# A one-core transformer block with a hand-kept order of work: one input load moved to GpSimd's DMA queue, and a new order list

## The chip, the cores and the metric

The kernel runs on one core of one Trainium2 chip. A core has TensorE (PE in the profile, with its weight loads PEld), VectorE (DVE), ScalarE (ACT), GpSimd (POOL) and SyncE (SP), each with its own instruction stream; they meet through semaphores. SP, ACT and GpSimd can issue DMA transfers, which run on the core's 16 DMA engines. The metric is the device time of one execution in microseconds (us); lower is better.

## The reference

A transformer block on x of 2048 tokens by 640 features, in bfloat16: layer norm, a memory-augmented linear and softmax attention of 32 heads of 20 features in 4 segments of 512 tokens, a residual, layer norm again, and a two-layer network with SiLU of 1728 hidden features.

```python
phi = lambda t: jnp.where(t > 0, t + 1.0, jnp.exp(t))
for s in range(N):                       # N = 4 segments of L = 512 tokens
    logits = einsum('bhqd,bhkd->bhqk', qs, ks) * scale + mask
    a_dot = einsum('bhqk,bhkd->bhqd', softmax(logits), vs)
    num = einsum('bhld,bhde->bhle', phi(qs), M)
    den = einsum('bhld,bhd->bhl', phi(qs), z)[..., None] + 1e-06
    outs.append(g * num / den + (1.0 - g) * a_dot)
    M = M + einsum('bhld,bhle->bhde', phi(ks), vs)
    z = z + einsum('bhld->bhd', phi(ks))
h = x + concat(outs) @ wo                # q, k, v from layernorm(x)
h2 = h + silu(layernorm(h) @ w1) @ w2
```

## The kernel before

The tokens are 16 blocks of 128 (x_tok holds 12 of them at a time), 4 blocks to a segment. Every piece of work is a task that `build` declares with what it reads and writes. `Graph.schedule` doesn't choose an order: it follows the text `ORDER` (line 360 on), a list of some 1,480 entries. An entry is a task's name, after a slash the engine where the task may run on several (A for ACT, D for DVE, G for GpSimd, S for SP), and after a colon the buffer places that it takes, such as the PSUM banks. Each engine executes its tasks in the order of the list, and `Tracker` puts a semaphore wait ahead of an instruction wherever an earlier task of another engine has to be done. So the list sets for every engine what stands behind what. The list was written by a search that works with a cost for each task; the kernel holds its result alone.

Names that matter here (the first digit after a name is the segment or the block, x and y are the first and the second half of segment 0):

- x0, x1, x2 (blocks 2 and 3 in one transfer), x4, x8: loads of x, line 577. w_q0, w_q1, w_k0, w_k1, w_wv0, w_wv1: loads of the projection weights, each in a part of 384 rows (0, from SP) and one of 256 rows (1, from ACT), line 580. beta: a small load with 128 copies, line 592.
- zpad, w2z, warm, halfc, epsc, epsg, mt, mta, mtb, mm, mzc, vpad: constants and masks, mostly on GpSimd. iota (line 629, GpSimd) and sel (line 631, DVE) make the identity matrix for transposes.
- fillN: N matmuls on zeros that only keep PE running (line 617).
- n1_st, n1_r, n1_ap: statistics (lines 737 and 740 on ACT, 745 and 748 on DVE), reciprocal root (lines 756 to 766) and application (line 772) of the first layer norm; n2_ the same for the second. n1_tp and n1_te (lines 781, 790): transpose on PE and its eviction in segment 0, called te0 to te3 below; n1_tr: transpose by DMA later.
- re_q, re_k (lines 695 and 697): the weights of q and k laid out by heads, in five parts c.
- pr, qe (lines 859, 867 and 868): projection of q (third digit 0) or k (1), and its eviction. ex, pha, phb (lines 874, 881, 887): phi.
- vt (line 899): twelve transfers that gather the heads of groups 5 to 7 from the projections into a place of their own.
- v, ve (lines 824, 834, 835): projection of v and its eviction.
- qk, e, mk (lines 936, 947, 958): scores of a group of four heads, the exponential, the causal mask. av, oe (lines 979, 992, 994): product with v and eviction. tn, nm (lines 1008, 1012, 1025 to 1045): transpose back, division. kt, mz, ma, mb: the memory M.
- ot, wo, rs (lines 1154, 1162, 1170): output projection and residual. h1, th, s (lines 1197, 1206, 1212) and h2, o, out (lines 1239, 1252, 1257): the network and the store.

SP's queue at the start issues x0, w_q0, w_k0, w_wv0, x4, w_wo, beta and then the weights of the network; ACT's queue issues x1, w_q1, x2, w_k1, w_wv1. The twelve vt go out on SP, some on ACT. The scores of groups 5, 6 and 7 in the first half (qk5x0, qk6x0, qk7x0) need all twelve; in the list, qk7x0 is the first of them, and v02 follows it on PE.

Which queue a load may take is an argument of its call:

```python
def load_x(b0, n, prio, bw=2.1, kind="plain", engs=(SP, AC)):
    s0 = b0 % 12
    dma(f"x{b0}", [], [(X[b], [0]) for b in range(b0, b0 + n)],
        lambda e: e.dma_start(out=x_tok[:, s0:s0 + n, :], in_=xv[:, b0:b0 + n, :]), prio, bw, kind, engs=engs)
```

Of the kernel before, what the change touches and what calls it, by code (L numbers as in the profile page):

```python
# [1314 lines left out]
```

## Time and profile before

| what | us |
|---|---|
| median of 3 runs (303.77 to 304.54) | 304.46 |
| the profiled execution, its own time | 305.88 |
| its span, first to last instruction | 304.1 |
| PE busy, of the span | 289.5 (95%) |
| ACT busy | 225.4 (74%) |
| DVE busy | 222.4 (73%) |
| GpSimd busy | 141.8 (47%) |

The granted clock of TensorE over the whole span is 0.994 of full speed. PE is the engine with the most work; matmuls are pipelined and their ends are modelled, so its busy time also holds short waits. Over the span of 304.1 us the page's slices show how PE and the clock stand, each digit a fortieth of the span in tenths:

```profile
PE   7799789999999999899999999999999999999996
...
PEclk9999799999999999999999999999999999999999
```

PE is below nine tenths in the first two slices, in the fifth and sixth (30.4 to 45.6 us), in the seventeenth and in the last; the clock is at 7 in the fifth (30.4 to 38.0 us). A row of the chain of waits (followed back from the last instruction) names the line and how long it held the chain; there PE has 73% of the span, DVE 11%, ACT 9%, and a DMA 3%, the load of wk at the start.

### The profile page before, as it was taken

Reading aid. Unit: us, or ns where it says so; the run is one execution under the profiler, and the core shown is the slowest. Engines: PE = TensorE matmul, PEld = TensorE weight load, DVE = VectorE, ACT = ScalarE, POOL = GpSimd, SP = SyncE. Lnnn points to the kernel's source line nnn. Section 1 sums busy time; section 2 is a strip of 40 time slices with the busy share of each in tenths; the row PEclk is TensorE's granted clock in tenths of the full one; section 3 lists DMA queues with packets and bytes.
Section 4 is the critical chain, followed back from the end, with each engine's and each line's share of the span. In section 5 each row is a group of like instructions: output and inputs, shape, how many; then the busy total and the mean of one; then the engine's idle time right before and its main releaser. Section 6 shows DMA issues by size and latency. Waiting matters only on the chain.

```text
span 304.1 us, 7512 instructions
## 1 busy us (share of the span) xinstructions
PE 289.5 (95%) x2989; PEld 171.4 (56%) x3011; DVE 222.4 (73%) x506; ACT 225.4 (74%) x326; POOL 141.8 (47%) x273
## 2 busy tenths in 40 slices
PE   7799789999999999899999999999999999999996
PEld 6575445465655555556654454466565547764574
DVE  5899777977749889989759876767874786745613
ACT  5899698999999899888679989886879841005400
POOL 7589543434545546765546437382855430300000
PEclk9999799999999999999999999999999999999999
DMA  7997415405344210151342300233230013240001
GB/s 264 358 369 118 87 24 138 114 19 162 72 101 95 43 34 10 34 107 27 64 134 76 67 19 19 39 64 75 65 68 24 0 20 68 45 122 9 0 30 58
DMA packets 48754, 24.66 MB, mean 81 GB/s; under 512 B 39184, under 2 KB 47632, under 8 KB 48720
## 3 DMA queue, kind: packets, MB, share of 16 engines
q1 hardware_dynamic: 46108, 21.06, 29.1%
q10 hardware_dynamic: 2612, 3.12, 3.6%
q8 instruction: 24, 0.39, 0.5%
q14 instruction: 10, 0.08, 0.1%
HBM read 10.41 MB, written 2.62 MB: 43 GB/s over the span
## 4 chain that ended last, share of the span: by engine, by line
PE 73%; DVE 11%; ACT 9%; DMA 3%; issue 2%; ACTq 1%; DVEq 0%
PE ps_all L1239 20%; PE ps_all L1197 16%; PE ps_all L859 9%; PE ps_all L824 7%; PE ps_all L936 6%; PE ps_all L1162 6%; ACT PT L947 6%; PE ps_all L979 4%; DMA sT<-in_A_wk_dram 3%; PE ps_all L1008 2%; PE ps_all L1101 2%; PE ps_all L1012 1%; DVE on L1045 1%; DVE sT L1212 1%; DVE x_tok L1170 1%
## 5 line engine op out<-in xcount | busy, mean ns | idle before, releaser
L947 ACT ACTIVATE PT<-ps_all 128x1024 bf16<-128x1024 f32 (+1 forms) x168 | 157.0, 990 | 17.2 <-PE ps_all L936 16.4
L958 POOL TENSOR_SCALAR_AFFINE_SELECT PT<-PT 128x512 bf16<-128x512 bf16 x128 | 82.4, 650 | 75.1 <-ACT PT L947 72.4
L1239 PE MATMUL ps_all<-w_sb,sT 128*128 128x320 bf16 (+2 forms) x462 | 64.6, 295 | 0.1
L1197 PE MATMUL ps_all<-hT,w_sb 128*128 128x512 bf16 (+1 forms) x315 | 60.3, 335 | 1.2 <-issue 1.0
L1206 ACT ACTIVATE th<-ps_all 128x512 f32<-128x512 f32 (+2 forms) x70 | 34.6, 510 | 34.2 <-PE ps_all L1191 19.6
L1239 PEld LDWEIGHTS ps_all<-w_sb,sT 128*128 128x128 bf16 x462 | 43.3, 98 | 19.2 <-issue 2.8
L1212 DVE SCALAR_TENSOR_TENSOR sT<-th,ps_all 128x512 bf16<-128x512 f32 (+2 forms) x70 | 37.8, 558 | 15.9 <-ACT th L1206 15.7
L1197 PEld LDWEIGHTS ps_all<-hT,w_sb 128*128 128x128 bf16 x325 | 29.9, 98 | 24.1 <-issue 2.6
L1252 DVE SCALAR_TENSOR_TENSOR x_tok<-ps_all,x_tok 128x640 bf16<-128x640 f32 (+3 forms) x18 | 13.4, 747 | 22.6 <-PE ps_all L1239 22.3
L745 DVE BATCH_NORM_STATS2 stt<-x_tok 128x6 f32<-128x320 bf16 x62 | 27.0, 477 | 0.8 <-DMA x_tok<-in_A_x_dram 0.5
L766 POOL TENSOR_TENSOR rst<-rst,eps_c 128x1 f32<-128x1 f32 x32 | 18.4, 576 | 12.7 <-DVE rst L760 10.6
L1162 PE MATMUL ps_all<-wo_sb,oT 128*128 128x320 bf16 x160 | 23.9, 299 | 0.0
L979 PE MATMUL ps_all<-PT,Vx 128*32 128x256 bf16 (+3 forms) x576 | 23.3, 287 | 0.5 <-DVE Vx L835 0.5
L1053 POOL TENSOR_TENSOR otok<-on 128x320 bf16<-128x320 bf16 x24 | 19.3, 810 | 7.8 <-DVE on L1045 7.8
L772 DVE TENSOR_SCALAR xn_rot<-x_tok,mvt,rst 128x640 bf16<-128x640 bf16 x32 | 15.7, 495 | 6.6 <-POOL rst L766 5.9
L868 DVE CAST QK<-ps_all 128x512 bf16<-128x512 f32 x24 | 16.5, 687 | 5.4 <-PE ps_all L859 5.1
L1045 DVE TENSOR_TENSOR on<-ps_all,rd 128x640 bf16<-128x640 f32 x24 | 19.8, 824 | 0.8
L1162 PEld LDWEIGHTS ps_all<-wo_sb,oT 128*128 128x128 bf16 x160 | 14.8, 98 | 7.2 <-issue 2.0
L824 PE MATMUL ps_all<-wv_sb,xT 128*128 128x320 bf16 x120 | 18.3, 299 | 0.3 <-ACT Vx L834 0.3
L979 PEld LDWEIGHTS ps_all<-PT,Vx 128*32 128x32 bf16 x576 | 12.2, 96 | 10.9 <-issue 4.1
L859 PE MATMUL ps_all<-xT,wqr 128*128 128x512 bf16 x68 | 17.2, 380 | 1.2 <-DVE x_tok L1170 0.7
L859 PE MATMUL ps_all<-xT,wkr 128*128 128x512 bf16 x70 | 17.6, 380 | 0.6 <-DVE sT L1212 0.2
(90 smaller groups left out, 350.7 us busy)
## 6 DMA issues: line engine op xcount, KB each, us to landing
w_sb<-in_B_w_dram SPq DMA_DIRECT2D x5, 432.0 KB, 11.0
x_tok<-in_A_x_dram SPq DMA_DIRECT2D x3, 640.0 KB, 10.5
out_dram<-x_tok SPq DMA_DIRECT2D x10, 160.0 KB, 1.8
w_sb<-in_B_w_dram SPq DMA_DIRECT2D x2, 480.0 KB, 3.8
wo_sb<-in_A_wo_dram SPq DMA_DIRECT2D x1, 800.0 KB, 12.3
out_dram<-x_tok ACTq DMA_DIRECT2D x5, 160.0 KB, 1.8
QKV<-QK SPq DMA_DIRECT2D x11, 72.0 KB
w_sb<-in_B_w_dram SPq DMA_DIRECT2D x1, 640.0 KB, 4.3
```

The lines of the kernel that those rows point to most:

```text
L745: T.add(DV, lambda e, hh=hh: e.bn_stats(out=stt[:, s, 6 * hh:6 * hh + 6], in_=xb[:, 320 * hh:320 * hh + 320]), reads=R((xa, xsub)), writes ...
L824: fns.append(lambda e, c=c, hh=hh: e.matmul(bank(ps, hh)[:, 0:320], lhsT=xT_[:, c, 128 * i:128 * i + 128], rhs=wv_sb[:, c, 320 * hh:320 * ...
L859: fns = [lambda e, kc=kc: e.matmul(bank(ps)[:, lo:hi], lhsT=wt[:, kc, c, :], rhs=xT_[:, kc, lo:hi], start=(kc == 0), stop=(kc == NC - 1)) ...
L947: T.add(AC, lambda e: e.activation(out=pt[:, pta.slot, q0:q0 + 2, 0:width], in_=sc3[:, b0:b0 + 2, 0:width], func=ACT.Exp, scale=SCALE), re ...
L958: T.add(PO, lambda e: e.affine_select(out=v, in_=v, pattern=[[0, 4], [1, 128]], compare_op=ALU.is_ge, fill=0.0, base=0, channel_multiplier ...
L979: fns.append(lambda e, j=j, r=r, h=h, pa=pa, pt=pt, co=co, q0=q0, ji=ji: e.matmul(bank(po)[32 * r:32 * r + 32, q0:hi], lhsT=Vx[:, vx.slot, ...
L1045: T.add(DV, lambda e: e.tensor_tensor(out=on[:, ona.slot, :, :].rearrange("p b (x e) -> p b x e", e=DH), in0=v[:, :, :, 0:DH], in1=r2.unsq ...
L1162: fns.append(lambda e, c=c, hh=hh: e.matmul(bank(ps, hh)[:, 0:320], lhsT=oT[:, c, 128 * i:128 * i + 128], rhs=wo_sb[:, c, 320 * hh:320 * h ...
L1197: fns = [lambda e, c=c: e.matmul(bank(ps)[:, lo:hi], lhsT=w1_sb[:, c, 128 * f:128 * f + 128], rhs=hT[:, c, lo:hi], start=(c == 0), stop=(c ...
L1206: T.add(AC, lambda e: e.activation(out=th[:, tha.slot, lo:hi], in_=bank(ps)[:, lo:hi], func=ACT.Tanh, scale=0.5), reads=R((ps, [0])), writ ...
L1212: T.add(DV, lambda e: e.scalar_tensor_tensor(out=sT[:, f, lo:hi], in0=th[:, tha.slot, lo:hi], scalar=1.0, in1=bank(ps)[:, lo:hi], op0=ALU. ...
L1239: fns.append(lambda e, f=f, t0=t0, fr=fr, hh=hh, n=n: e.matmul(bank(pa, hh)[:, 0:n], lhsT=sT[:, f, t0:t0 + 128], rhs=w2_sb[:, fr, c0 + 320 ...
```

## The change

The load of x2 and x3 (blocks 2 and 3, 320 KB) is issued by GpSimd in place of ACT; it is GpSimd's first task. The whole list is replaced by another result of the search, in which the issue times of transfers are taken as they were measured, and in which VectorE and GpSimd take their turns in order of time. The tasks are the same ones, except for the filler matmuls: 55 in four groups in place of 38 in three. What changes is their order on each engine, the engine of tasks that can run on several (n1_st0, for one, moves from ACT to DVE, and oe goes to ACT 8 times in place of 14), and the PSUM banks and other places. The diff of the list is cut to its start, as far as qk7x0, and its end.

```diff
--- before.py
+++ after.py
@@ -358,108 +358,108 @@
      "x0": -0.6, "xs": 0.4, "y0": 3.0, "ys": 0.65, "wox": 3.6, "h1x": 5.0}
 
 ORDER = """
-x1:3 mt1:0 mt0 halfc x0:7 w_q1:0 x2:5,0 mta0 mtb0 mm2 mm9 w_q0 w_k0 mt3 w_wv0:0 x4:1,2,4,6 iota w_wo:0 beta w2z/D:0
-zpad w_w2_4 w_w1_2:0 w_w1_4 w_w2_5 epsc sel mta3 vpad1 w_k1 w_wv1 x8/S:8,9,10,11 warm n1_st0/A:1,0 vpad0 mtb3 mm8
-n1_st1/D:6 n1_r1/D n1_ap1:1 mta1 w_w1_1 re_wq1/A:0 re_wq0/D n1_r0/G n1_ap0:0 re_wq2/D epsg0 n1_st3/D:0 mtb1 mm3 mt2
-mta2 mm11 mm1 n1_r3/G mtb2 n1_st2/D:2 n1_r2/D n1_ap3:2 re_wk1/D:0 n1_ap2:3 w_w1_0 w_w1_3 re_wk4/D re_wk3/D re_wq3/D
-fill6:0 fill27:1 fill5:2 mm7 mm6 mm4 mm5 mm10 mm0 n1_tp1:0 n1_te1/A:0 re_wk2/D n1_tp0:4 n1_te0/A pr020x:7 pr000x:2
-pr010x:0 re_wq4/A n1_tp3:3 re_wk0/A pr001x:5 qe000x/A:0 qe010x/A:0 qe020x/A:0 n1_te3/A qe001x/A n1_tp2:0 n1_te2/A
-pr011x:2 qk0x0:3 pr040y:7 pr001y:0 qe011x/D e0x0:0 e0x2 mk0x_0 qe001y/D qe040y/A:0 qk1x0:1 e1x0:1 pha001:2 mk0x_256
-e1x2 mk1x_0 pr021x:5 qe021x/D pr041y:6 qe041y/A pr031y:0 n1_st5:3 n1_r5/G n1_st4:7 n1_r4/G n1_ap5:3 n1_tr5:0
-qe031y/A:0 ex001:1 phb001 kt00:1 mk1x_256 pr030x:1 qe030x/A qk2x0:4 e2x2:2 zf0 zf1 mzc10 mzc0 mzc8 mzc9 mzc6 mzc4 mzc5
-mzc3 lsc0 mzc2 pr041x:2 pr031x:3 qe031x/D qe041x/D e2x0 pha031:1 mzc1 lsc1 mk2x_0 pha041:0 n1_ap4:1 mzc7 epsg1 mzc11
-ex031:1 mk2x_256 pr040x:0 qe040x/A pr030y:1 qe030y/D vt07/S:0 vt011/S vt02/S n1_st6:5 vt01/S lsc2 lsc3 n1_r6/G vt08/S
-n1_st11:2 n1_r11/G n1_st10:0 qk3x0:2 e3x2:3 pr010y:6 e3x0 pr011y:7 qe011y/D phb031 vt05/A n1_ap6:0 n1_st7:4 mk3x_0
-mk3x_256 n1_ap11:2 qe010y/A n1_st9:1 n1_r10/G pr000y:0 qe000y/A qk4x0:2 e4x2:5 pr021y:1 vt04/A pr020y:6 qe021y/A
-pha021:2 e4x0 mk4x_0 qe020y/A mk4x_256 ex041:0 vt00/S vt06/S v00:4 ve00/A:0 qk0yb0:0 e0yb2:4 vt09/A v01:6 n1_r9/D
-vt010/S e0yb0 vt03/A ve01/A mk0yb_0 ex011:2 n1_r7/G n1_tr6 n1_tr4 v03:4 ve03/D qk1yb0:0 e1yb0:6 av0x:6 oe0x/D:1 av4x:4
-av2x:7 e1yb2 mk1yb_0 mk1yb_256 tn0x:0 oe4x/D:0 oe2x/D:1 ex021:1 phb021 kt02:0 nm0x:0 n1_st8:6 n1_ap7:1 n1_tr7 qk7x0:1
-e7x0:2 v02:5 n1_r8/D n1_ap9:0 phb041 tn4x:7 nm4x:0 e7x2 mk7x_0 mk7x_256 ve02/A qk5x0:1 av1x:0 v11:5 e5x0:0 e5x2 mk5x_0
...
-s3_5_0 h2_15_0_2:2 th3_4_0:0 th3_10_0:1 s3_4_0 s3_10_0 h1_3_9_0:5 th3_9_0:1 s3_9_0 h1_3_7_0:4 th3_7_0:0 h1_3_8_0:1
-th3_8_0:1 h2_13_0:6 s3_7_0 h2_15_0_1:0 h2_15_1_1 s3_8_0 h2_15_2_1 h2_15_3_1 o15_1 out15_1/S h2_15_0_0:3 h2_13_1
-h2_13_2 h2_13_3 o13 out13/A h2_15_1_0 h2_15_1_2 h2_14_0:4 h2_14_1 h2_14_2 h2_12_0:0 h2_14_3 h2_12_1 o14 out14/S
-h2_12_2 h2_12_3 o12 out12/S h2_15_2_0 h2_15_3_0 o15_0 out15_0/S h2_15_2_2 h2_15_3_2 o15_2 out15_2/A
+x0:7 w_q0:0 x1:3 w_q1 x2:5,0 epsg0:0 mt2 mt0 zpad iota w_k0 w_wv0:0 vpad0 x4:1,2,4,6 w2z/D:0 mta0 mtb0 mm0 w_wo:0 beta
+w_w2_4 w_w1_1:0 w_w1_2 w_w1_4 halfc w_w1_0 w_k1 w_wv1 w_w2_5 sel warm n1_st0/D:1,0 w_w1_3 x8/S:8,9,10,11 n1_st1/D:6
+mm6 epsc n1_r0/G n1_ap0:0 mm2 re_wq1/D:0 n1_r1/G n1_ap1:1 mt3 mta3 n1_st3/D:0 mt1 mm9 n1_r3/G mta1 mtb1 mm5 n1_st2/D:2
+mm1 n1_r2/G mm4 mm3 mtb3 mm8 vpad1 mta2 re_wq0/A re_wq2/A mtb2 mm10 mm11 fill42:0 n1_tp0:2 n1_tp1:4 re_wk0/D:0
+n1_ap3:2 re_wq4/D n1_te1/A:0 n1_te0/A mm7 re_wk1/A re_wq3/D re_wk2/A re_wk4/A n1_ap2:3 fill10:1 pr000x:4 pr010x:1
+pr011x:0 qe011x/A:0 qe010x/D n1_tp3:2 n1_te3/D re_wk3/D n1_st5:3 n1_r5/G n1_st6:5 n1_r6/G n1_st4:7 n1_r4/G qe000x/A:0
+pr001x:5 qe001x/A pr020x:7 qe020x/A:0 n1_tp2:0 n1_te2/A qk0x0:2 e0x2:0 pr021x:6 e0x0 mk0x_0 qe021x/A pr001y:7 qe001y/A
+pha001:2 n1_ap5:3 n1_tr5:0 pr041y:0 qe041y/A:0 qk1x0:1 e1x0:1 ex001:1 phb001 lsc0 zf0 zf1 mzc9 mzc2 mzc0 mzc8 lsc1
+mzc3 mzc6 mzc5 mzc7 mk0x_256 mzc10 mzc1 pr030x:5 qe030x/D:0 mzc4 e1x2 kt00:1 n1_st7:4 mk1x_0 mk1x_256 mzc11 n1_ap6:0
+pr040y:6 pr030y:0 qe030y/A pr041x:7 qe041x/A pha041:0 pr031x:1 qe040y/A epsg1 qk2x0:2 pr031y:0 lsc2 e2x0:2 qe031y/A
+qe031x/A e2x2 mk2x_0 pr040x:7 qe040x/D vt02/S:0 pr010y:6 qk3x0:0 e3x0:3 e3x2 vt01/A mk2x_256 n1_st9:1 qe010y/D vt08/S
+vt07/S mk3x_0 mk3x_256 pr021y:7 vt010/S qe021y/D ex021:1 pr011y:4 vt05/S qe011y/D pr000y:5 qk4x0:0 e4x2:5 e4x0 mk4x_0
+vt04/A n1_st11:2 ex041:0 qe000y/D pr020y:4 qe020y/D vt00/S vt06/S n1_r11/G vt03/A vt09/S n1_st8:6 n1_r8/G n1_r9/G
+v00:6 ve00/D:0 mk4x_256 pha021:2 pha011:1 phb021 qk0yb0:2 e0yb0:4 v01:0 e0yb2 mk0yb_0 mk0yb_256 vt011/A ex011:2 kt02:0
+n1_tr6 n1_r7/D ve01/D v03:6 phb041 lsc3 ve03/D qk1yb0:2 e1yb0:6 av2x:1 av0x:0 oe0x/D:1 oe2x/D:0 av4x:7 e1yb2 mk1yb_0
+tn0x:6 nm0x:0 n1_ap4:1 n1_ap11:2 mk1yb_256 n1_st10:0 n1_ap7:3 qk7x0:0 v02:4 oe4x/A:1 tn4x:6 av1x:7 oe1x/D:1 n1_tr7
+e7x0:2 e7x2 mk7x_0 n1_ap9:0 mk7x_256 nm4x:0 n1_r10/G pha031:2 ve02/A qk5x0:0 e5x0:0 e5x2 v11:4 mk5x_0 mk5x_256 ex031:1
+n1_tr4 qk6x0:0 tn1x:7 phb011 e6x2:1 e6x0 mk6x_0 mk6x_256 nm1x:3 fill3:6 tn2x:6 nm2x:1 av7x:7 ve11/A:1 oe7x/D:1 av3x:6
...
+th3_5_0:1 s3_5_0 h1_3_6_0:4 th3_6_0:0 h1_3_8_0:5 th3_8_0:1 s3_6_0 h1_3_12_0:7 h2_14_0:0 h2_15_0_1:3 h2_15_1_1 s3_8_0
+h2_15_2_1 h2_15_0_2:2 th3_12_0:0 s3_12_0 h2_15_1_2 h2_15_3_1 o15_1 out15_1/A h2_14_1 h2_14_2 h2_14_3 o14 out14/S
+h2_13_0:4 h2_13_1 h2_13_2 h2_13_3 h2_15_0_0:6 o13 out13/S h2_12_0:0 h2_12_1 h2_12_2 h2_15_1_0 h2_12_3 o12 out12/S
+h2_15_2_0 h2_15_3_0 o15_0 out15_0/A h2_15_2_2 h2_15_3_2 o15_2 out15_2/S
 """.split()
@@ -582,7 +582,7 @@
     cw = lambda w: w.rearrange("(c p) e -> p c e", p=128)
     load_x(0, 1, -100, 2.30, "fix", (SP,))
     load_x(1, 1, -100, 2.33, "fix", (AC,))
-    load_x(2, 2, -97, 4.79, "fix", (AC,))
+    load_x(2, 2, -97, 4.79, "fix", (PO,))
     for wi, (k, A_w) in enumerate((("q", A_wq), ("k", A_wk))):
         load_w(k + "0", wraw[:, wi, 0:3, :], cw(A_w[0:384, :]), -99, 4.0, [(sT0, [k + "0"])], "fix", (SP,))
         load_w(k + "1", wraw[:, wi, 3:5, :], cw(A_w[384:640, :]), -99, 2.7, [(sT0, [k + "1"])], "fix", (AC,))
```

More of the change, by code (lines that the diff above doesn't have):

```diff
@@ new lines @@
+qk0ya0:0 e0ya2:5 oe3x/D:0 tn7x:7 nm7x:2 tn3x:4 nm3x:1 mz00:5 ma00/A:0 mb00:0 kt01:1 av5x:6 oe5x/D:0 av6x:7 e0ya0
+qk1ya0:2 oe6x/D:1 tn5x:6 nm5x:3 tn6x:7 nm6x:0 ot1:0 e1ya2:0 phb031 ot0 v10:0 ve10/D e1ya0 qk2ya0:4 e2ya0:2 av0y:2
+oe0y/D:1 v12:0 e2ya2 qk2yb0:2 e2yb0:1 w_w2_0/A ve12/D e2yb2 mk2yb_0 mk2yb_256 wo1:6 qk3ya0:0 e3ya2:3 rs1 n2_st1:5
+wo0:4 tn0y:7 nm0y:1 e3ya0 rs0 n2_st0:3 n2_r1/G n2_ap1:3 n2_tr1:0 n2_r0/G n2_ap0:1 n2_tr0 av1y:6 oe1y/A:0 qk4ya0:0
+pr101:7 v13:5 mz02:4 e4ya0:4 e4ya2 qe101/A:0 ma02/D:3 mb02:0 ve13/D pha101:1 ex101:2 phb101 qk3yb0:0 e3yb2:5 pr120:7
@@ new lines @@
+pha230:0 e16e0:5 e16e2 vt210/S vt24/S vt25/S vt211/S pha240:0 v22:6 ve22/D pha231:0 ex240:2 phb240 ex230:0 phb230
+vt22/S vt21/S vt28/S h1_0_13_1:0 th0_13_1:1 phb231 s0_13_1 mk16e_0 mk16e_256 qk17b0:2 e17b0:3 h1_0_11_1:1 th0_11_1:0
+s0_11_1 wo6:6 e17b2 mk17b_0 mk17b_384 qk18b0:0 e18b2:0 e18b0 mk18b_0 mk18b_384 rs6 ex220:0 av16:5 oe16/D:1 wo7:6
+n2_st6:6 qk17a0:2 e17a2:6 rs7 n2_r6/G n2_st7:4 e17a0 mk17a_0 wo4:0 rs4 n2_ap6:2 vt27/S ex241:2 h1_0_9_1:6 h1_0_3_1:7
+th0_9_1:1 th0_3_1:0 qk18e0:2 n2_r7/D s0_3_1 s0_9_1 wo5:0 e18e0:1 e18e2 mk18e_0 mk18e_256 phb220 n2_ap7:0 rs5
@@ new lines @@
+ad16 h1_1_7_0:3 th1_4_0:0 s1_4_0 phb241 th1_7_0:1 mk21b_384 s1_7_0 qk20a0:4 x12/S e20a2:0 e20a0 mk20a_0 h1_1_1_0:1
+n1_st12:0 h1_1_12_0:2 n1_r12/G th1_1_0:1 s1_1_0 th1_12_0:0 s1_12_0 n1_ap12:1 n1_tr12:0 mz23:0 qk20e0:3 h1_1_5_0:7 ma23
+e20e2:4 e20e0 mk20e_0 kt21:0 n1_st13:3 th1_5_0:1 h1_1_11_0:1 th1_11_0:0 n1_r13/G mk20e_256 s1_11_0 s1_5_0 qk21a0:3
+e21a2:1 e21a0 h1_1_2_0:2 th1_2_0:1 mk21a_0 n1_st14:6 n1_r14/G h1_1_6_0:0 th1_6_0:0 s1_2_0 n1_ap13:0 n1_tr13 n1_st15:1
+n1_ap14:2 n1_tr14 h1_1_8_0:1 qk22a0:4 e22a2:2 th1_8_0:1 s1_6_0 e22a0 v30:2 ve30/A:1 n1_r15/G n1_ap15:3 n1_tr15 mk22a_0
@@ new lines @@
+h1_1_0_0:6 th1_0_0:0 s1_8_0 s1_0_0 av21:7 av20:5 qk22b0:0 mz21:4 ma21 oe21/A:1 tn21:6 nm21:1,1 ad21 kt20:0 e22b0:3
+e22b2 mk22b_0 mk22b_384 oe20/D:1 h1_1_9_0:4 th1_9_0:1 s1_9_0 qk23a0:0 v32:6 ve32/D e23a0:6 e23a2 pr300:5 qk22e0:0
+e22e0:1 mk23a_0 qe300/D:0 pha300:0 e22e2 mk22e_0 mk22e_256 pr310:4 tn19:6 qe310/D:0 ex310:1 ex300:2 mz20:5 ma20
+pr301:0 qk23b0:2 e23b2:0 nm19:2,0 e23b0 mk23b_0 mk23b_384 phb300 mb20:0 pr311:1 ad19 qe301/D h1_1_3_0:7 th1_3_0:0
+kt24:0 tn20:5 qe311/D s1_3_0 qk24e0:1 e24e0:4 e24e2 mk24e_0 nm20:1,1 ad20 mk24e_256 pr320:0 pr330:7 v33:1 qe320/D:0
@@ new lines @@
+n2_ap13:3 n2_tr13:0 n2_ap14:2 n2_tr14 n2_ap15:1 n2_tr15 h2_8_1 h2_8_2 h2_8_3 wo12:4 o8 out8/A h2_9_0:0 rs12 n2_st12:7
+n2_r12/G h2_9_1 h2_9_2 h2_9_3 n2_ap12:0 n2_tr12 o9 h2_11_0:2 h2_11_1 h2_11_2 h2_11_3 o11 h2_10_0:0 h2_10_1 h2_10_2
+h2_10_3 out9/S h1_3_13_0:3 o10 out10/A out11/S th3_13_0:0 s3_13_0:0 h1_3_11_0:2 h1_3_0_0:5 th3_11_0:1 s3_11_0
+th3_0_0:0 h1_3_3_0:6 th3_3_0:1 s3_0_0 s3_3_0 h1_3_4_0:4 th3_4_0:0 s3_4_0 h1_3_9_0:0 th3_9_0:1 s3_9_0 h1_3_2_0:1
+h1_3_10_0:2 th3_2_0:1 h1_3_1_0:7 th3_1_0:0 s3_2_0 s3_1_0 th3_10_0:1 s3_10_0 h1_3_7_0:3 th3_7_0:0 s3_7_0 h1_3_5_0:6
```

136 lines of the change are left out of this document (55 added, 81 removed).

## The prediction

> **What bounds the kernel now.** I read the busy times by stage first (us of the stage, then busy us of PE, PEld, DVE, ACT, POOL, granted clock, DMA share, GB/s).
>
> ```profile
> 0.00:10.00 10.00, 7.00 (x54) 5.53 (x55) 5.84 (x17) 5.95 (x13) 6.78 (x32) 1.00 0.85 288
> 10.00:20.00 10.00, 9.39 (x104) 7.10 (x103) 9.10 (x35) 9.33 (x23) 6.89 (x18) 1.00 1.04 355
> 20.00:30.00 10.00, 9.25 (x101) 5.68 (x99) 9.79 (x31) 9.18 (x18) 9.34 (x28) 1.00 0.87 194
> 30.00:40.00 10.00, 7.71 (x101) 4.03 (x101) 7.57 (x23) 7.25 (x12) 6.09 (x11) 0.83 0.34 72
> ...
> 28.50:31.91 3.41, 1.74 (x38) 0.78 (x36) 3.14 (x9) 2.87 (x5) 2.97 (x7) 0.98 0.65 120
> 31.91:35.33 3.42, 3.23 (x20) 1.77 (x20) 2.64 (x10) 1.51 (x2) 1.23 (x2) 0.52 0.44 92
> ```
>
> From 10 to 30 us three engines are full, DVE most of all (9.10 and 9.79 of 10). In 30 to 40 all of them fall, and the clock is 0.83. The last two rows narrow it: 3.4 us in which PE is busy for 1.74, then 3.4 us at about half the clock. After 40 us PE is busy for 256.15 of 264 us (289.50 less the four rows above), and 2.8 of the 7.9 us that are left are the last evictions and stores after 301.33. So what a new order can win lies in the first 40 us, and some 5 us are spread thinly over the rest.
>
> Next the timeline at that hole (start, us, engine, line, operation; in brackets the idle time before it and its releaser).
>
> ```profile
> 28.63 0.79 SPq L899 DMA_DIRECT2D w_sb<-w_sb  x1
> ...
> 30.44 0.25 PE L1012 MATMUL ps_all<-ident,oTs 128*128 128x84 bf16 x2
> ...
> 32.07 0.16 PEld L936 LDWEIGHTS ps_all<-w_sb 20*128 20x128 bf16 x8 [1.52 <-DMA w_sb<-w_sb]
> 32.10 0.51 PE L936 MATMUL ps_all<-w_sb 20*128 20x256 bf16 x8 [1.41 <-DVE rd L1025]
> ...
> 32.54 2.82 PE L824 MATMUL ps_all<-wv_sb,hT 128*128 128x320 bf16 x10
> ```
>
> The scores of head group 7 (qk7x0, L936 at 32.10) need the last of the twelve transfers that gather the extra heads (vt010, issued at 28.63: 3.44 us from issue to use), and a bank that DVE frees. Behind it v02 (L824) runs at half clock: 2.82 us, where ten of its kind take 1.53 at 24.35.
>
> Last, the start: when data lands and who waits.
>
> ```profile
> 2.36 0.24 POOL L629 IOTA iot<- 128x128 int32 x1
> 2.64 1.67 DVE L631 TENSOR_SCALAR ident<-iot 128x128 bf16<-128x128 int32 x1 [0.91 <-POOL iot L629]
> 3.82 0.89 DVE L745 BATCH_NORM_STATS2 stt<-x_tok 128x6 f32<-128x320 bf16 x2
> ...
> 8.93 0.89 DVE L745 BATCH_NORM_STATS2 stt<-x_tok 128x6 f32<-128x320 bf16 x2 [0.49 <-DMA x_tok<-in_A_x_dram]
> ```
> ```profile
> sT<-in_A_wq_dram ACTq DMA_DIRECT2D x1, 320.0 KB, 4.9
> x_tok<-in_A_x_dram ACTq DMA_DIRECT2D x1, 320.0 KB, 7.2
> sT<-in_A_wk_dram ACTq DMA_DIRECT2D x1, 320.0 KB, 8.4
> ```
>
> x2/x3 land 7.2 us after issue (1.72), at 8.92, and DVE's statistics start at 8.93. The second part of wk lands at 10.70 and the first exponential of scores (e0x0) starts at 13.87. From 2.5 us on the loads move 355 to 391 GB/s in nearly every slice of the first 14 us, so the queues share a full path.
>
> **The change, part by part. 1, x2/x3 from GpSimd.** It is GpSimd's first instruction, so epsg0, mt2, mt0 and iota wait behind it, DVE's sel waits for iota, and the statistics stand behind sel. The trace has no DMA issued there. Bounds of its hold: 0.54 us (the same transfer's issue on ACT's queue) and 3.96 (the beta load on SP's, the longest issue). I take 1.0, nearer to the like transfer. Then iota ends at 0.78 + 1.0 + 0.33 (three memsets, some 0.11 from start to start) + 0.24 = 2.35, against 2.60: no loss. Zero at a hold of 1.25; above it the start slips us for us, up to 2.7. The transfer stands first in its queue. Bounds: 2.8 us (160 KB on an empty queue) to 11.0 (640 KB on SP's queue in the first 14 us). Between wq's 320 KB behind 160 KB (4.9) and the 7.2 of now I take 5.8 after a descriptor start near 1.3: landing at 7.1. The 320 KB that move ahead take up to 0.9 us (320 KB at 369 GB/s) from the others: wq lands at up to 7.0 instead of 6.1. ACT's queue has one transfer less, and wk's second part takes x2's place: 8.92 to 9.8, not 10.70.
>
> The Trainium skill (SBUF — State Buffer, section "SBUF: two separate sides") warns of just this queue: GpSimd can't write a DMA's descriptors while VectorE runs an instruction that takes the port they share. The trace of before can't show it. By that rule the two memsets that DVE runs until 1.73 could hold this DMA, and the case priced as second rival below would be the likelier.
>
> **2, the order of the start.** x0's statistics move from ACT (1.77 us there, 4.79 to 6.56) to DVE, and re_wq0, re_wq2 to ACT. DVE now waits for x0 (0.79 + 2.8 = 3.6) and sel: first statistics at 4.0, the second at 5.05 (start to start 1.05, as at 8.93 and 9.98), first apply at 6.15, re_wq1 at 7.0 (wq), second apply to 7.85, x3's statistics at 7.85 instead of 8.93. So x2 has 0.75 us of cover; landing later than 7.85 costs DVE us for us. ACT: re_wq0 and re_wq2 (0.81 each) from 7.0 to 8.6, two transpose evictions (0.70 each) to 10.0, so the first projections start at 10.05 instead of 9.36; three re_wk (2.5) to 12.5, four qe (0.26 from start to start) and te2 (0.71) to 14.3. The first exponential is at 14.3 to 14.5, 0.5 later. Seventeen more filler matmuls (0.11 us each) end near 7.5, before PE has anything to do.
>
> **3, from there to qk7x0.** Counting the list, ACT has to e4x2 one qe more than before (+0.27), and from there to e7x0 two qe, one ex and two ve fewer and one oe more: -0.52 - 0.55 - 1.35 + 0.4 = -2.0. So ACT can start e7x0 at about 30.1; it had ended its part at 31.37. DVE takes what ACT gave. To the end of oe2x (31.29 now) it has more: x0's statistics 1.05, ve00 and ve01 1.48, te3 0.74, one qe 0.36, one phb 0.42; less: re_ 1.0, two applies 0.9, two small ones 0.3, one oe 0.45. Sum +1.4. Against that stand idle times now: 2.15 us between 4.95 and 8.93, of which 0.4 stays, less 0.2 for the later start: 1.55. By this DVE ends oe2x at 31.1. My chain of starts for the new order, each at the spacing of its row, gives 31.45; I take 31.3. The transfers: after qe020y only vt00, vt06 and vt09 are left for SP (0.83 from start to start), where four were. With qe020y at 25.9 the last issue starts at 27.6, plus 3.44 is 31.05. So DVE's bank comes last, and qk7x0 starts at about 31.45: -0.6.
>
> **4, the clock.** With PE filled to about 31.2 the window that now holds 1.74 us of 3.41 would hold more, and I take it that the half clock falls away: v02 costs 1.5, not 2.8: -1.3. Without that, 0.
>
> The Trainium skill (TensorE: Matmul & The Clock Gate, section "What's actually happening") says that the clock falls after an idle window of about 3.4 us. The trace agrees with the length (3.41) but not with idle: PE was busy in half of the window.
>
> **5, the rest of the list.** 40 to 301: PE's work is the same; about 5 us of gaps. Over the run some 6 us of row time move from ACT to DVE (oe: ACT 14 to 8, DVE 26 to 32). From 60 to 100 ACT is busy for 39.13 of 40 us and DVE for 29.50, so the cover is there; from 100 to 140 DVE has 35.57. I take 0, bounds -1.5 and +2. The tail: the last eviction (0.28) and store are of the same size: 0.
>
> Sum: -0.6 - 1.3 = -1.9. The profiled run took 305.88 (span 304.1 and 1.8 around it), so 304.0 for such a one; the median of the runs is 304.46, 1.4 below it, and I put the change on that: **302.6**.
>
> **The rivals.** *No change.* The half clock comes back in another window, since PE's share near 30 us stays at two thirds, and other waits eat 0.6: 304.4. For: the same row shows that half a window of work isn't enough. Against: ACT and SP are both ahead.
>
> *GpSimd holds the start.* The DMA occupies GpSimd, or lands late, and sel, DVE's statistics and with them the full DVE chain up to qk7x0 slip. At the upper bound +2.7 on 31.45: qk7x0 at 34.15, +2.05, and v02 again at half clock: 306.5. It decides from a hold of 1.25 + 0.65 = 1.9 us, or a landing after 8.5. For: POOL's first 2.6 us now hold iota. Against: the like issue is 0.54.
>
> *DVE is the bound.* DVE idles in the new order as much as now (0.90 + 0.21 us in 10 to 30), oe2x ends at 32.4, the hole and the half clock stay (+0.4), and from 100 to 140 us one of its 1.84 us of PE gaps (38.16 of 40) comes twice (+0.9): 305.8. It decides once DVE loses over 0.7 us more than I took.
>
> **How the numbers follow.** Forecast 0.45, no change 0.18, GpSimd 0.18, DVE 0.19. What a measurement can tell from no change is 0.3%, 0.9 us: faster is below 303.55, slower above 305.37. Of the forecast's own range, 300.9 (part 5's -1.5) to 304.0, nearly all is faster; with a little of the others: faster 0.46, same 0.19, slower 0.35. For 8 in 10 I reach from 300.7 to 306.6.
>
> **What would show it.** x2 landed by 7.9 us; iota done by 2.7; first exponential at 14.3 to 14.6; no wait of PE over 0.5 us ahead of qk7x0, which starts before 31.7; clock 1.0 in 30 to 40 us; PE's busy time over 60 to 260 within 2 us of now. I am wrong if sel ends after 4.5, if DVE has gaps between 10 and 30 us, or if the half clock is there.

## The result, and the profile after

The changed kernel takes 307.42 us (median of four runs, 307.18 to 307.62) where the kernel before takes 304.37 beside it (303.77 to 304.54): a ratio of 1.0104, 95% interval 1.0086 to 1.0121. It is slower by 3 us. In a second comparison on another chip it took 306.71 against 305.45, 1.0047 (1.0023 to 1.0071); with 11 and 28 runs against four and four, that is the better measure of the size. All ratios are taken from the fast runs, while the medians in the table further down hold every run, three slow ones too (307.24 of a_x8first, 313.01 of a_x8e_beta and 726.99 us of a_x8e_act). The prediction was 302.6.

The busy times by stage of the changed kernel, in the columns of before; the last two rows are stretches chosen by hand.

```profile
0.00:10.00 10.00, 8.51 (x64) 6.69 (x65) 6.15 (x18) 4.21 (x8) 6.25 (x27) 1.00 0.84 283
10.00:20.00 10.00, 8.79 (x91) 6.65 (x88) 9.19 (x33) 9.14 (x25) 8.39 (x27) 1.00 1.05 366
20.00:30.00 10.00, 6.58 (x66) 4.60 (x67) 6.76 (x21) 6.33 (x12) 6.64 (x20) 0.93 0.83 165
30.00:40.00 10.00, 8.92 (x107) 4.97 (x105) 8.72 (x23) 6.91 (x12) 7.49 (x15) 0.90 0.37 63
24.74:27.87 3.13, 0.01 (x2) 0.00 (x0) 2.10 (x7) 0.35 (x1) 1.65 (x3) 1.00 0.47 98
28.60:32.05 3.45, 3.45 (x21) 1.62 (x20) 2.76 (x9) 1.94 (x4) 2.21 (x6) 0.51 0.43 54
```

Between 20 and 30 us all engines lose about 3 us against before (PE 6.58 for 9.25, DVE 6.76 for 9.79, ACT 6.33 for 9.18). The fifth row finds it in one piece: 3.13 us in which PE does nothing. Half the clock follows in the sixth, as it did before, only earlier.

What each engine waited for there, from the timeline (the brackets hold the idle time before the row and its releaser):

```profile
8.49 3.79 SPq L580 DMA_DIRECT2D w_sb<-in_B_w_dram  x7
12.33 0.43 SPq L577 DMA_DIRECT2D x_tok<-in_A_x_dram  x1
...
22.19 0.41 DVE L868 CAST w_sb<-ps_all 128x256 bf16<-128x256 f32 x1
25.74 0.89 DVE L745 BATCH_NORM_STATS2 stt<-x_tok 128x6 f32<-128x320 bf16 x2 [3.14 <-DMA x_tok<-in_A_x_dram]
...
27.52 0.63 ACT L874 ACTIVATE ex<-w_sb 128x512 bf16<-128x512 bf16 x1 [3.49 <-DVE w_sb L868]
27.87 0.72 PE L859 MATMUL ps_all<-hT,wqr 128*128 128x256 bf16 x5 [3.13 <-DVE w_sb L868]
```

Read it from the bottom. PE needs a bank that one of DVE's evictions frees (qe011y, L868); ACT needs what another of them writes; DVE is not busy but stands at the statistics of block 9 (n1_st9, L745), which wait for x8, the load of blocks 8 to 11. SP issued x8 at 12.33, behind seven loads of network weights. Before, it stood behind four and was issued at 10.22, and the first statistics that need it (block 11) came at 22.80 without a wait:

```profile
7.94 2.24 SPq L580 DMA_DIRECT2D w_sb<-in_B_w_dram  x4
...
10.22 0.59 SPq L577 DMA_DIRECT2D x_tok<-in_A_x_dram  x1
10.85 2.54 SPq L580 DMA_DIRECT2D w_sb<-in_B_w_dram  x3
...
22.80 0.87 DVE L745 BATCH_NORM_STATS2 stt<-x_tok 128x6 f32<-128x320 bf16 x2
```

The changed kernel's chain of waits has the load as one row:

```profile
12.33 13.38 DMA x_tok<-in_A_x_dram
```

It lands 13.38 us later, at 25.71. In the new list w_w1_1, w_w1_0 and w_w1_3 stand ahead of x8, n1_st9 stands on DVE ahead of the five evictions qe010y to qe020y, and n1_st11 ahead of the last two. The late load and the early n1_st9 together close DVE's queue for 3.14 us.

The start, which the change is named after:

```profile
1.32 0.92 POOL L577 DMA_DIRECT2D x_tok<-in_A_x_dram  x1 [0.82 <-POOLq L1300]
2.62 0.25 POOL L629 IOTA iot<- 128x128 int32 x1
2.90 0.81 DVE L631 TENSOR_SCALAR ident<-iot 128x128 bf16<-128x128 int32 x1 [1.18 <-POOL iot L629]
3.66 0.89 DVE L745 BATCH_NORM_STATS2 stt<-x_tok 128x6 f32<-128x320 bf16 x2
...
8.58 0.89 DVE L745 BATCH_NORM_STATS2 stt<-x_tok 128x6 f32<-128x320 bf16 x2 [0.79 <-DMA x_tok<-in_A_x_dram]
```
```profile
sT<-in_A_wq_dram ACTq DMA_DIRECT2D x1, 320.0 KB, 5.7
x_tok<-in_A_x_dram POOLq DMA_DIRECT2D x1, 320.0 KB, 7.2
sT<-in_A_wk_dram ACTq DMA_DIRECT2D x1, 320.0 KB, 8.4
```

GpSimd is held for 0.92 us and the first statistics start at 3.66, so the hold does no harm here; but x2/x3 land 7.2 us after issue, as they did from ACT's queue.

### The profile page after: what moved, and what is told of

Read it like the earlier page. It is cut to its first block, busy times and chain, and to the rows that moved or that the text cites. A ratio compares the mean times of both kernels' runs of the same rounds, so it can differ in the third digit from the quotient of the medians.

```text
span 305.5 us, 7572 instructions
## 1 busy us (share of the span) xinstructions
PE 293.6 (96%) x3028; PEld 173.8 (57%) x3028; DVE 224.0 (73%) x511; ACT 220.6 (72%) x317; POOL 142.9 (47%) x277
## 4 chain that ended last, share of the span: by engine, by line
PE 79%; ACT 6%; DVE 5%; DMA 4%; SPq 4%; issue 1%; DVEq 0%; ACTq 0%
PE ps_all L1239 20%; PE ps_all L1197 17%; PE ps_all L859 10%; PE ps_all L936 7%; PE ps_all L1162 7%; PE ps_all L824 7%; PE ps_all L979 5%; DMA x_tok<-in_A_x_dram 4%; ACT PT L947 4%; PE ps_all L1008 2%; SPq L580 2%; PE ps_all L1012 2%; PE ps_all L1101 1%; SPq L592 1%; DVE Vx L835 1%
## 5 line engine op out<-in xcount | busy, mean ns | idle before, releaser
L1197 PE MATMUL ps_all<-hT,w_sb 128*128 128x512 bf16 (+1 forms) x325 | 62.6, 337 | 0.0
L1252 DVE SCALAR_TENSOR_TENSOR x_tok<-ps_all,x_tok 128x640 bf16<-128x640 f32 (+3 forms) x18 | 13.4, 748 | 25.0 <-PE ps_all L1239 24.8
L745 DVE BATCH_NORM_STATS2 stt<-x_tok 128x6 f32<-128x320 bf16 x64 | 28.0, 478 | 4.5 <-DMA x_tok<-in_A_x_dram 4.1
L1162 PE MATMUL ps_all<-wo_sb,oT 128*128 128x320 bf16 x160 | 24.1, 299 | 0.0
L994 DVE TENSOR_SCALAR oTs<-ps_all,lsc 128x512 bf16<-128x512 f32 (+1 forms) x32 | 19.7, 627 | 2.1 <-PE ps_all L979 2.0
L868 DVE CAST QK<-ps_all 128x512 bf16<-128x512 f32 x24 | 16.4, 686 | 3.6 <-PE ps_all L859 3.2
L1162 PEld LDWEIGHTS ps_all<-wo_sb,oT 128*128 128x128 bf16 x160 | 14.7, 98 | 7.4 <-issue 2.2
L824 PE MATMUL ps_all<-wv_sb,xT 128*128 128x320 bf16 x120 | 18.3, 299 | 0.6 <-ACT Vx L834 0.4
L859 PE MATMUL ps_all<-xT,wkr 128*128 128x512 bf16 x75 | 18.7, 380 | 0.0
L859 PE MATMUL ps_all<-xT,wqr 128*128 128x512 bf16 x75 | 18.5, 380 | 0.0
```

The costliest lines, as they stand in the source:

```text
L745: T.add(DV, lambda e, hh=hh: e.bn_stats(out=stt[:, s, 6 * hh:6 * hh + 6], in_=xb[:, 320 * hh:320 * hh + 320]), reads=R((xa, xsub)), writes ...
L824: fns.append(lambda e, c=c, hh=hh: e.matmul(bank(ps, hh)[:, 0:320], lhsT=xT_[:, c, 128 * i:128 * i + 128], rhs=wv_sb[:, c, 320 * hh:320 * ...
L859: fns = [lambda e, kc=kc: e.matmul(bank(ps)[:, lo:hi], lhsT=wt[:, kc, c, :], rhs=xT_[:, kc, lo:hi], start=(kc == 0), stop=(kc == NC - 1)) ...
L1162: fns.append(lambda e, c=c, hh=hh: e.matmul(bank(ps, hh)[:, 0:320], lhsT=oT[:, c, 128 * i:128 * i + 128], rhs=wo_sb[:, c, 320 * hh:320 * h ...
L1197: fns = [lambda e, c=c: e.matmul(bank(ps)[:, lo:hi], lhsT=w1_sb[:, c, 128 * f:128 * f + 128], rhs=hT[:, c, lo:hi], start=(c == 0), stop=(c ...
```

## The experiments

Three theories. **Theory 1**: x8's load comes too late for n1_st9, which stands ahead of evictions on DVE. **Theory 2**: GpSimd's queue costs the time at the start. **Theory 3**: the new list is slower further back. The kernel before ran beside each set on the same chip; ratios are against it. "Lower clock" counts the runs whose mean granted clock was 0.994 or less, which is what a stretch of 3.4 us at half clock makes of it; the kernel before has it in 46 of 120 runs.

| run | median us | ratio (95% interval) | lower clock |
|---|---|---|---|
| a_x8early | 303.25 | 0.9931 (0.9902 to 0.9960) | 4 of 11 |
| a_stlate | 304.55 | 0.9968 (0.9945 to 0.9991) | 1 of 12 |
| a_x2act | 306.98 | 1.0039 (1.0011 to 1.0066) | 9 of 12 |
| b_x2pool | 305.58 | 1.0005 (0.9980 to 1.0029) | 7 of 12 |
| a_again | 306.71 | 1.0047 (1.0023 to 1.0071) | 9 of 11 |
| b_x8late | 306.47 | 1.0039 (1.0016 to 1.0062) | 5 of 12 |
| a_x8e_act | 303.52 | 0.9950 (0.9918 to 0.9982) | 3 of 12 |
| a_x8e_beta | 308.09 | 1.0071 (1.0045 to 1.0097) | 6 of 6 |
| a_fill | 306.66 | 1.0050 (1.0026 to 1.0074) | 1 of 12 |
| a_x8e_fill | 303.31 | 0.9950 (0.9927 to 0.9973) | 0 of 12 |
| a_x8first | 303.40 | 0.9960 (0.9929 to 0.9991) | 3 of 12 |
| b_fill | 304.61 | 0.9970 (0.9950 to 0.9990) | 0 of 12 |
| a_x8early2 | 303.79 | 0.9944 (0.9917 to 0.9972) | 5 of 12 |
| a_x8e_act2 | 303.74 | 0.9952 (0.9922 to 0.9981) | 4 of 12 |

**a_x8early: the load in its old place.** In the changed list, three names move:

```diff
-w_w2_4 w_w1_1:0 w_w1_2 w_w1_4 halfc w_w1_0 w_k1 w_wv1 w_w2_5 sel warm n1_st0/D:1,0 w_w1_3 x8/S:8,9,10,11 n1_st1/D:6
+w_w2_4 w_w1_2:0 w_w1_4 halfc w_k1 w_wv1 w_w2_5 sel warm n1_st0/D:1,0 x8/S:8,9,10,11 w_w1_1 w_w1_0 w_w1_3 n1_st1/D:6
```

> The changed kernel with one edit: in the list, three of the w1 loads stand behind the load of blocks 8 to 11 on SyncE's queue again, as in the kernel before; x2 and x3 stay with GpSimd, all else in the list stays. Theory 1 (the load of blocks 8 to 11 comes too late for VectorE's statistics of block 9, which stand ahead of the evictions): the load lands by about 22, VectorE's idle time of 3.14 us at 22.6 and TensorE's of 3.13 us at 24.7 go down to under 0.5, and the time falls by 2.5 to 3.5 us to about 304 to 305. Theory 2 (GpSimd's queue costs the time at the start): the hole may close, but the time stays at 306.5 to 307.5. Theory 3 (the list is slower further back): the same, 306.5 to 307.5.

The timeline of this kernel:

```profile
8.19 2.21 SPq L580 DMA_DIRECT2D w_sb<-in_B_w_dram  x4
...
10.45 0.59 SPq L577 DMA_DIRECT2D x_tok<-in_A_x_dram  x1
11.08 2.38 SPq L580 DMA_DIRECT2D w_sb<-in_B_w_dram  x3
...
22.41 0.89 DVE L745 BATCH_NORM_STATS2 stt<-x_tok 128x6 f32<-128x320 bf16 x2 [0.17 <-DMA x_tok<-in_A_x_dram]
```

The same statistics start at 22.41 and DVE waits 0.17 us instead of 3.14. The time is 1.2% under the changed kernel's ratio of 1.0047, some 3.5 us, and under the kernel before. Theory 1 holds; 2 and 3 fall, since both left this kernel at 306.5 or more. It is also 0.75 us under the 304 that I had as the lower end; where that comes from is under "Where the time went".

**a_stlate: the load stays late, the statistics move.**

```diff
-... mk2x_256 n1_st9:1 qe010y/D ... vt04/A n1_st11:2 ex041:0 qe000y/D pr020y:4 qe020y/D vt00/S
+... mk2x_256 qe010y/D ... vt04/A ex041:0 qe000y/D pr020y:4 qe020y/D n1_st9:1 n1_st11:2 vt00/S
```

> The changed kernel with one edit: the statistics of blocks 9 and 11 stand behind the four evictions of the first group's y part on VectorE, not ahead of them; the load of blocks 8 to 11 stays as late as it is. Theory 1: the load still lands near 25.7, but VectorE's evictions no longer wait for it; TensorE's hole of 3.13 us goes to under 1, and the time falls to 304 to 305.5. A theory in which the late load itself costs (its bandwidth, or SyncE's queue) has the time at 307. Theories 2 and 3: 306.5 to 307.5.

PE's hole of 3 us is gone (the longest wait left is 1.13 at 29.7) and 304.55 is as expected. So most of the cost isn't the late transfer itself, but the instruction that waits for it at the head of DVE's queue. Part of the delay moved: n1_st9 now starts at 25.85 ahead of ve00, the eviction of v's first block, which comes at 28.87 (27.09 in a_x8early), and this kernel's median stays 1.3 us behind a_x8early's (the two intervals overlap by a little).

**a_x2act and b_x2pool: the queue alone, both ways.** Each changes one argument:

```diff
-    load_x(2, 2, -97, 4.79, "fix", (PO,))
+    load_x(2, 2, -97, 4.79, "fix", (AC,))
```

> The changed kernel with x2 and x3 loaded from ScalarE's queue again, its list as it is. Theory 1: VectorE still waits about 3 us for the load of blocks 8 to 11, the time stays within 0.7 us of 307.4. Theory 2 (the third queue costs): the time falls to 304 to 305.5. If the third queue is worth what I predicted of it at the start, it is slower by 0 to 0.7.

> The kernel before with x2 and x3 loaded from GpSimd's queue, its list as it is (three short memsets stand ahead of the load on GpSimd). Theory 1: no harm, 303.7 to 305 against 304.4; the load issues about 0.3 us behind where the changed kernel has it. Theory 2: 306 to 307.5, with the first exponential later by 1 us or more.

Back on ACT's queue the changed kernel is no faster beyond the intervals (1.0039 against 1.0047); DVE waits for x8 there too, until 25.58. On GpSimd's queue the kernel before is where it was (1.0005). Theory 2 falls from both sides.

**a_again and b_x8late.** a_again is the changed kernel unedited. b_x8late does the harm alone, in the kernel before: x8/S moves behind w_w1_3.

> The changed kernel once more, so that it stands beside the other edits on one chip. If the wait of 3.14 us is always there: 306.5 to 309, with the clock of TensorE at 0.994 in the mean (a stretch of about 3.4 us at half clock) in nearly all runs, where the kernel before had it in 12 of 34.

> The kernel before with one edit: the load of blocks 8 to 11 stands behind the three w1 loads on SyncE's queue, as in the changed kernel; nothing else moves. Theory 1: it issues 2.2 to 2.5 us later and lands near 25; VectorE's statistics of block 11, which start at 22.8 in the kernel before, wait until then, what stands behind them comes 2 to 3 us later, and the time rises by 1.5 to 3.5 us, with half clock in more runs than before. If the place of the load is not the cause: within 0.7 us of the kernel before.

```profile
8.24 3.79 SPq L580 DMA_DIRECT2D w_sb<-in_B_w_dram  x7
...
12.08 0.43 SPq L577 DMA_DIRECT2D x_tok<-in_A_x_dram  x1
...
24.90 0.89 DVE L745 BATCH_NORM_STATS2 stt<-x_tok 128x6 f32<-128x320 bf16 x2 [1.51 <-DMA x_tok<-in_A_x_dram]
```

The place of the load costs the old order too, 0.39% or 1.2 us, with a wait of 1.51 us: less than the 1.5 to 3.5 that I expected, since DVE came to the first statistics that need x8 (block 11) only at 23.39. The new list asks for block 9 at 22.6, so the same place costs it more. Half clock came in no larger share of the runs (5 of 12, 13 of 28 in the kernel before beside it), against what I expected.

**a_x8e_act, then a_x8early2 and a_x8e_act2 side by side: what the third queue is worth.** The list of a_x8early with x2 and x3 from ACT or from GpSimd.

> The changed kernel with the load of blocks 8 to 11 ahead of the w1 loads, and x2 and x3 from ScalarE's queue: the new list without the third queue and without the wait. The list's start waits for x3's statistics, 1.5 us later in the trace with ScalarE's queue than with GpSimd's. If that now carries through: 1 to 1.7 us more than the 302.9 of the same list with GpSimd's queue, 303.9 to 304.6 at full clock. If the start is hidden behind something else: the same 302.9.

> The changed kernel with the load of blocks 8 to 11 ahead of the w1 loads, once more, beside the next: 302.5 to 303.6, 0.5 to 1.0% under the kernel before.

> The same with x2 and x3 on ScalarE's queue. If the third queue brings something: 0.4 to 0.8 us over the run beside it. If it brings nothing: within 0.3 us of it.

303.79 with GpSimd's queue (0.2 us over what I expected) and 303.74 with ACT's: nothing that can be measured. a_x8e_act ran beside a_again, 303.52 against 306.71. In a_x2act's profiled execution the statistics of block 3 began at 9.94, 1.4 us later than in the changed kernel's; that was that execution's own, for in these two with ACT's queue they begin at 8.32 and 9.00. Over all profiled executions here, x2/x3 land 6.6 to 8.2 us after issue from ACT (six, mean 7.3) and 6.7 to 8.2 from GpSimd (ten, mean 7.3); the issue starts 0.4 us sooner on GpSimd, the rest is spread. The Trainium skill (DMA: Bandwidth & Descriptors, section "Issuing engines are not separate DMA queues") says that transfers of all engines end up on the same 16 DMA engines and interleave, so that another issuer saves only the time to issue; the 7.3 and 7.3 agree.

**a_x8e_beta and a_x8first: can x8 come sooner still?** In a_x8e_beta `beta` moves behind x8, in a_x8first x8 stands right behind beta.

> The changed kernel with the load of blocks 8 to 11 ahead of the w1 loads and beta's broadcast load, whose issue holds SyncE for 3.4 us, behind it. Theory: the load of blocks 8 to 11 issues 3.4 us earlier, near 7.0, but the transfers ahead of it fill the queues, so that it lands only 0.5 to 3 us earlier; the time is the same or up to 0.7 us less than with the first edit alone (302.2 to 302.9 at full clock), unless beta now comes too late for ScalarE's exponentials of beta at 18.0 (then VectorE and ScalarE stall there, 303.5 or more).

> The changed kernel with the load of blocks 8 to 11 right behind beta, ahead of all w1 and w2 loads (in the first edit a w2 load, two w1 loads and a shorter w2 load stood ahead of it). It issues some 2.2 us earlier, near 8.2, and lands 1 to 2.5 us earlier, near 20 to 21. If the load still set something in the first edit (VectorE's statistics of block 9 began at its landing, 22.38): 0.2 to 0.5 us less than 302.9 at full clock. If it was early enough: the same 302.9.

The timeline of a_x8e_beta:

```profile
4.68 5.05 SPq L580 DMA_DIRECT2D w_sb<-in_B_w_dram  x4
9.78 0.59 SPq L577 DMA_DIRECT2D x_tok<-in_A_x_dram  x1
10.41 1.59 SPq L592 DMA_DIRECT2D beta_bc<-in_A_beta_dram  x1
...
21.90 0.23 ACT L635 ACTIVATE bsel<-beta_bc 128x32 f32<-128x32 bf16 x1 [3.84 <-DMA beta_bc<-in_A_beta_dram]
```

It was the bad branch of what I expected: beta came too late for ACT. What I hadn't seen is why x8 gained so little. The hold of SP near 5 us isn't beta's own: when beta leaves that place, four weight loads take 5.05 us there instead of 2.21, and beta takes 1.59 instead of 3.1 to 4.9 in the others. So x8 gained 0.7 us, not 3.4, and beta's 8 KB, which land 11.5 and 11.6 us after issue in the two places, came 3.84 us too late for ACT. a_x8first gained nothing either: in its profile n1_st9 starts at 22.97, and 303.40 is a_x8early's time. Where x8 stood before is early enough.

**a_fill, a_x8e_fill, b_fill: what the half clock costs.** Matmuls on zeros in places where PE waits. They take free banks and change nothing that is computed.

```diff
 a_fill:     ... qe011y/D pr000y:5 +fill18:0 qk4x0:0 e4x2:5 ...
 a_x8e_fill: ... e1yb0:6 +fill6:0 av2x:1 ... n1_ap7:3 +fill3:2 qk7x0:0 ...
 b_fill:     ... n1_ap7:1 n1_tr7 +fill10:5 qk7x0:1 ...
```

> The changed kernel with one addition: 18 matmuls on zeros (128x256, some 0.11 us apart, together about 2 us; their sum goes nowhere) on TensorE right ahead of the scores of group 4, in the hole in which TensorE waits 2.4 to 3.1 us for VectorE. VectorE's wait for the load stays. If the half clock in 9 of 11 runs comes from that hole, it is gone in nearly all runs and the median falls by about 1 us, to the 305.7 that the two runs at full clock had; the 0.9 us by which these are over the kernel before at full clock stay. If the half clock comes from elsewhere: the same share of runs and the same time, 306.7.

> The changed kernel with the load of blocks 8 to 11 ahead of the w1 loads, and 6 and 3 matmuls on zeros on TensorE near 29.9 and 32.2, where it waits 1.02 us for VectorE and 0.47 us for a transfer. If the half clock of 4 runs in 11 of that kernel starts from this thin stretch (0.68 us busy of 1.7 at 29.9 and 1.19 of 1.7 at 31.6), it goes to at most 1 in 11 and the median falls from 303.25 to about 302.9; if the added matmuls get in the way, the time at full clock rises over 302.9 by 0.3 to 1.

> The kernel before with one addition: 10 matmuls on zeros (some 1.1 us) on TensorE near 30.7, in the 1.41 us for which it waits ahead of the scores of group 7. If the half clock itself costs the 1.3 to 1.5 us by which runs with it were slower: the share of runs with it goes from 36 of 91 to under 1 in 10, and the mean of all runs falls by 0.4 to 0.6 us under that of the kernel before. If it only goes with slow runs: it goes, the runs at full clock now reach up to 307, and the mean stays within 0.2 us.

In all three the half clock goes almost entirely (1, 0 and 0 of 12 runs). In the kernel before that is worth what the prediction read: its ratio is 0.9970, the mean of all runs 304.63 against 305.30, and none reaches over 305.32 (before: 306.77). The windows of b_fill, cut where the prediction cut those of before, and its timeline:

```profile
28.50:31.91 3.41, 2.96 (x50) 1.94 (x49) 3.09 (x9) 3.17 (x6) 2.97 (x7) 1.00 0.65 129
31.91:35.33 3.42, 3.21 (x44) 1.86 (x42) 3.32 (x12) 2.69 (x5) 1.87 (x3) 1.00 0.42 86
```
```profile
31.00 1.26 PE L617 MATMUL ps_all<-zpad 128*128 128x256 bf16 x10
32.19 0.34 PE L936 MATMUL ps_all<-w_sb 20*128 20x256 bf16 x8
32.46 1.53 PE L824 MATMUL ps_all<-wv_sb,hT 128*128 128x320 bf16 x10
```

PE is busy for 2.96 of 3.41 us instead of 1.74, the clock stays at 1.00, and v02 (L824) takes 1.53 us instead of 2.82. In the changed kernel the same remedy moved nothing (306.66 against 306.71, where I expected 305.7), and in a_x8e_fill nothing beyond the interval (303.31, where I expected 302.9). Why is open: a_fill's profiled execution is level with a_again's at group 7 (35.67 and 35.80) and then loses 0.8 us between 42 and 60 us, 0.43 of it ahead of L1162 for a transposing transfer and 0.40 ahead of L936 for ACT; whether the other runs do so was not seen.

**Where the time went.** Start times of some instructions in three profiled executions at full clock (b_fill stands for the kernel before):

| us | b_fill | a_again | a_x8early |
|---|---|---|---|
| statistics of block 3 (x2/x3 landed) | 9.37 | 8.95 | 8.21 |
| exponential e0x2 of group 0 (the second there before, the first in the new list) | 15.02 | 15.38 | 14.64 |
| eviction qe020y | 25.59 | 28.68 | 25.73 |
| exponential of group 7, e7x0 | 32.65 | 35.80 | 32.97 |
| output row o1 (L1252) | 93.31 | 96.59 | 93.76 |
| output row o2 | 148.79 | 149.79 | 146.95 |
| output row o12 | 299.07 | 300.33 | 297.85 |

At e7x0 the changed kernel is 3.15 us behind and a_x8early 0.32; both carry it on to o1. The 0.32 is the best of its kind: in the six profiles with x8 early again (a_x8e_beta apart), e7x0 starts at 32.97 to 34.39, and at 32.27 to 32.72 in the three of the old list with x8 in place. Between o1 and o2 both regain 2.3 us (3.28 to 1.00, and 0.45 to -1.84), and this is no matter of the execution: that stretch takes 53.19 to 53.21 us in the twelve profiles of the new list and 55.44 to 55.48 in the four of the old. Behind o2 the new list gives some of it back (0.3 us in a_again, 0.6 in a_x8early). One row of before and one of a_again show where over half of the 2.3 is won:

```profile
100.00:140.00 40.00, 38.16 (x445) 22.52 (x442) 35.57 (x77) 36.05 (x51) 22.91 (x36) 1.00 0.24 46
```
```profile
100.00:140.00 40.00, 39.45 (x460) 22.70 (x459) 35.10 (x80) 37.95 (x54) 24.35 (x40) 1.00 0.26 49
```

PE is busy for 39.45 us there instead of 38.16. So theory 3 is the reverse of the truth: the list is better further back. From e7x0 to o12 it takes 264.53 us in a_again and 264.88 in a_x8early against 266.42, so it wins 1.5 to 1.9 us there; in a_again that hid more than half of the 3.15 that it had lost by group 7.

## Why the prediction was wrong

**Part 1, x2/x3 from GpSimd: right on the hold, wrong on the landing.** The hold is 0.92 us (taken: 1.0); iota ends at 2.87 (2.35), since the issue starts at 1.32 and not at 0.78; and the first statistics start at 3.66 (4.0). The landing was taken at 7.1 because the transfer stands first in its queue; its statistics start at 8.58 in the profile and at 8.07 to 9.52 in all. The bounds covered it, and the working's own remark, that the queues share a full path, was the better guide. The second part of wk lands at 10.13, not by 9.8. Whether DVE's memsets held GpSimd's issue is not shown: the second ran until 1.73, 0.41 us into the issue, whose 0.92 us are 0.38 more than the like issue on ACT; in b_x2pool the issue takes 0.95 with an overlap of 0.34. The landing is no later for it, 7.2 us from either queue.

**Part 2, the order of the start: right in its spacing, late by part 1's landing.** The first projections come at 9.78 (10.05). The first exponential was to start at 14.3 to 14.6; it is e0x2 in the new list, and it starts at 15.01, 1.14 us after the first one before (e0x0, 13.87). It was to follow the statistics of block 3 by 6.45 us (7.85 to 14.3) and follows them by 6.43 (8.58 to 15.01), and by 6.26 to 6.50 in all twelve profiles of the new list. So the miss is the landing's.

**Part 3, from there to qk7x0: the step that failed.** It counted the instructions that DVE gains and loses, and took DVE's idle time as known: "2.15 us between 4.95 and 8.93, of which 0.4 stays". It never named x8. The diff moves three weight loads ahead of it on SP and two statistics that need it ahead of evictions on DVE; with the rows at hand (x8 issued at 10.22, the three loads behind it issued in 2.54, 640 KB 11.0 us from issue to landing) that gave a landing near 23.8 and a stall. Measured: it landed at 25.71, since it took 13.38 us from issue; DVE ran out at 22.6 and waited 3.14 us; and e7x0 came 4.45 us later than in the profile before, where -0.6 was forecast:

```profile
32.72 1.51 ACT L947 ACTIVATE PT<-ps_all 128x768 bf16<-128x768 f32 x2 [1.36 <-PE ps_all L936]
```
```profile
37.17 1.51 ACT L947 ACTIVATE PT<-ps_all 128x768 bf16<-128x768 f32 x2 [0.16 <-PE ps_all L936]
```

Part of the 4.45 is half clock, which the changed kernel has ahead of e7x0 and the kernel before mostly behind it; at full clock in both it is 3.15 (35.80 against 32.65). The sign that the text had set against itself, gaps of DVE between 10 and 30 us, is what came.

With x8 put back, -0.6 is still too much: a_x8early, the earliest of its kind, starts e7x0 at 32.97 against 32.65. The chain there ends in the gathers, as the working had it, but the last is issued at 29.39, not at 27.6: when qe020y was done, near 26.1, SP still had five to issue and not three.

**Part 4, the clock: the size was right, what it was taken from was wrong.** Half clock costs the kernel before 1.3 us in a run that has it (v02 2.82 and 1.53). But the working took 1.3 off the median, 304.46, and most runs under that median hadn't got it: the profiled run was 1.4 above the median, and runs with half clock are 1.4 to 1.5 slower than those without in all four sets. A gain from removing it could only be booked against 305.88, or against the median at the share of runs that have it: 46 of 120 times 1.4 us, 0.5 us. And it didn't go away in the changed kernel; the hole brought it in all four of the first runs and in 9 of 11 later.

**Part 5, the rest of the list: taken as 0, measured at -1.5 to -1.9** from e7x0 to o12, at the bound of -1.5 or past it, with -2.3 between o1 and o2 alone. The working had the row (38.16 of 40 us busy) and used it for a rival on the slow side alone.

So 302.6, which a_x8early nearly meets (303.25 and 303.79), would have been right by luck, for wrong reasons: -0.6 and -1.3 didn't come, and part 5 gave -1.5 to -1.9 where 0 was taken.

**The rivals.** *No change* is out. *GpSimd holds the start* had set a landing after 8.5 as its sign, and 8.58 just meets it; but it is out as the cause, since the landing is as late from ACT's queue and the queue alone changes nothing measurable in either kernel. *DVE is the bound* had the right engine and the idle time that it put at 0.7 us or more, but not the cause: DVE lacked data, not time. No rival held a late load, and the range ended at 306.6.

## What to carry to other kernels

When an order is changed, go through the loads first: for each queue, what now stands ahead of each transfer, when it lands, and which instruction is the first to need it; an in-order engine that meets that instruction early stops everything behind it, however little work it has. A third issuing queue was worth nothing here, where the transfers already filled the shared path (355 to 391 GB/s in nearly every slice before). And when a profiled run lies off the median, find out why before a term is taken from the one and booked on the other.
